# Which engine waits for the landing of the output: GpSimd or SyncE, in a one-core decode kernel

## The chip, the cores and the metric

The kernel runs on one core of a Trainium2 chip and gives instructions to five engines: TensorE (PE), VectorE (DVE), ScalarE (ACT), GpSimd (POOL) and SyncE (SP). They run side by side: the busy times of the first four, 58.4, 44.2, 30.4 and 10.0 us in the profile below, add up to 143.0 us in a span of 77.6. Where one waits for another in this kernel, it waits for a semaphore, a counter that the other raises; SyncE's longest such wait is 28.5 us. The metric is the device time of one execution in microseconds; quoted times are medians of several executions. Before the change it is 79.57 us (three runs, 79.53 to 79.73).

Besides the device time there is a profile. Its "span" runs from the first to the last of the kernel's own instructions that were recorded. The device time is about 2 us longer than the span (79.66 us against 77.6 in the profiled run), and this case is about those 2 us.

## The reference

One decode step: a layer norm, then an attention over a window of 4096 cached positions and a gated feed-forward block, both added to the input. Cut to what matters:

```python
x  = A_x                                  # 1 x 1 x 512, bf16
xn = _layernorm(x)
q  = xn @ wq                              # 32 heads of 128
scores = q @ k_cache[last 4096].T * Dh**-0.5
o  = softmax(scores) @ v_cache[last 4096] # 8 kv heads, each used by 4 heads
a  = o @ wo                               # 512 numbers
b  = xn + ((silu(xn @ w_gate) * (xn @ w_up)) @ w_down) * sigmoid(xn @ w_r)
return x + a + b                          # 1 x 1 x 512: 1 KB
```

About 30.7 MB are read from memory and 1 KB is written.

## The kernel before

The change touches only the last line of the body. This is the helper that gives waits to engines (cut), the helper that issues a transfer, and the end of the kernel:

```python
class Eng:
    ...
    def need(self, *toks):               # this engine waits for each (semaphore, value)
        for t in toks:
            ...
                self.e.wait_ge(sem, n)

    def dma(eng, name, out_, in_):
        s = S("d_" + name)
        ins = eng.dma_start(out=out_, in_=in_)
        ins.then_inc(s, 16)              # 16: the value that need() waits for
        ...
        return (s, 16)
    ...
    t_a = PE.mark(ins)                   # the last matrix product
    DVE.need(t_a)
    ACT.need(t_a)
    s_res = S("s_res")
    ve.tensor_copy(out=res[:, 0:HD], in_=g_ps[0]).then_inc(s_res, 1)
    ac.copy(out=res[:, HD:], in_=g_ps[1]).then_inc(s_res, 1)
    sy.wait_ge(s_res, 2)
    t_out = dma(sy, "out", out.rearrange("a b d -> (a b) d"), res)
    POOL.need(t_out)                     # keeps the kernel open until the output has landed
```

The framework's usual closing barrier is moved by this kernel to an early place in each engine's stream (a function `hoist`, not shown): in the trace GpSimd's semaphore instructions for it stand at 6.37 to 6.90 us of the span. So at its end an engine just falls through its last branch, which I call the **closing branch**. The wait of the last line is compiled into the closing branch of the engine that has it: in the trace this branch of GpSimd, with the wait on it, runs from 77.559 to 77.592 us, behind the landing at 77.534.

Of the kernel before, what the change touches and what calls it, by code (L numbers as in the profile page):

```python
# [38 lines left out]
def kernel(  # L39
# [63 lines left out]
    def early(eng, name, out_, in_):  # L103
# [81 lines left out]
    PE, ACT, DVE, POOL, SP = (Eng(nc, nc.tensor, "pe"), Eng(nc, nc.scalar, "act"), Eng(nc, nc.vector, "dve"),  # L185
                              Eng(nc, nc.gpsimd, "pool"), Eng(nc, nc.sync, "sp"))
# [10 lines left out]
# [3 lines that stand above are left out]
        ins.then_inc(s, 16)  # L200
        if name == "v0":
            ends(ins)
        return (s, 16)
# [365 lines left out]
    ac.copy(out=res[:, HD:], in_=g_ps[1]).then_inc(s_res, 1)  # L569
    sy.wait_ge(s_res, 2)  # L570
    t_out = dma(sy, "out", out.rearrange("a b d -> (a b) d"), res)
    POOL.need(t_out)


# [28 lines left out]
```

## Time and profile before

| | before |
|---|---|
| device time, median of 3 | 79.57 us |
| device time of the profiled run | 79.66 us |
| span of the profiled run | 77.6 us |
| from issue to landing of the output | 1.12 us |
| from landing to the end of device time | 2.13 us |

The last two rows are from the trace's records of semaphore updates. The store's semaphore is updated twice, at 76.851 and 77.534; the later one, 25 ns ahead of the branch that waits for it, is what I call the landing. In the profile's page, the first lines give each engine's busy time, with its share of the span, and what the transfers moved in 40 slices of the span:

```profile
PE 58.4 (75%) x642; PEld 30.6 (39%) x642; DVE 44.2 (57%) x96; ACT 30.4 (39%) x41; POOL 10.0 (13%) x22
...
DMA  6999999999999999999999999999999999989900
...
DMA packets 2745, 30.72 MB, mean 396 GB/s; under 512 B 307, under 2 KB 438, under 8 KB 822
```

The transfers fill 37 slices of 40, and GpSimd, with 13%, is the least busy engine. The last 1.2 us of the span, as busy time of each engine in two windows, show that nothing works there any more:

```profile
76.40:77.00 0.60, 0.00 (x0) 0.00 (x0) 0.00 (x0) 0.00 (x0) 0.00 (x0) 1.00 0.00 0
77.00:77.60 0.60, 0.00 (x0) 0.00 (x0) 0.00 (x0) 0.00 (x0) 0.00 (x0) 1.00 0.01 2
```

The columns are the window, its length, busy time and number of instructions of PE, PEld, DVE, ACT and POOL, then the granted clock, the transfers' share and GB/s.

### The profile page before, as it was taken

What the parts mean: (1) busy time and instruction counts of PE and PEld (TensorE: products, weight loads), DVE (VectorE), ACT (ScalarE), POOL (GpSimd) and SP (SyncE); (2) the same over time, 40 slices, a digit from 0 to 9 for tenths busy, and PEclk for the clock granted to TensorE, in tenths of its full rate; (3) what the DMA queues carried; (4) which work ended last, traced back from release to release, by engine and by line L of the source; (5) the groups of instructions that cost most, each with busy time, mean ns of one, the idle gap of its engine ahead of it and who ended that gap; (6) DMA issues with size and microseconds to landing.
All of it is one profiled execution on the core that took longest, in us unless ns stands there. A gap on an engine that the chain in (4) does not pass through costs nothing.

```text
span 77.6 us, 1640 instructions
## 1 busy us (share of the span) xinstructions
PE 58.4 (75%) x642; PEld 30.6 (39%) x642; DVE 44.2 (57%) x96; ACT 30.4 (39%) x41; POOL 10.0 (13%) x22
## 2 busy tenths in 40 slices
PE   0010797759997997997996796677887889898891
PEld 0010401346785575765864234222222344243240
DVE  2763910177656956868883652989879545600302
ACT  2760101404397698599568016143333322000001
POOL 3950000001020210201205900000000000000000
PEclk9999999999999999999999999999999999999999
DMA  6999999999999999999999999999999999989900
GB/s 136 405 406 422 414 422 427 422 469 414 439 456 439 405 422 414 439 439 431 405 410 422 481 414 422 413 449 399 451 406 451 413 422 414 481 361 413 355 29 1
DMA packets 2745, 30.72 MB, mean 396 GB/s; under 512 B 307, under 2 KB 438, under 8 KB 822
## 3 DMA queue, kind: packets, MB, share of 16 engines
q1 hardware_dynamic: 2738, 30.67, 94.0%
q8 instruction: 2, 0.03, 0.2%
q14 instruction: 1, 0.01, 0.0%
q10 hardware_dynamic: 4, 0.00, 0.0%
HBM read 30.67 MB, written 0.00 MB: 395 GB/s over the span
## 4 chain that ended last, share of the span: by engine, by line
DMA 64%; PE 20%; ACT 6%; DVE 4%; issue 2%; SPq 1%
DMA k_sb<-in_B_w_down_dram 50%; DMA wq_sb<-in_A_wq_dram 14%; PE ps L367 10%; ACT kT L342 6%; PE ps L541 3%; PE ps L376 3%; PE ps L295 2%; DVE kin L334 2%; PE ps L307 1%; SPq L199 1%; DVE kT L339 1%; DVE qpad L312 1%; DVE kT L568 1%; SPq L84 0%; SPq L101 0%
## 5 line engine op out<-in xcount | busy, mean ns | idle before, releaser
L342 ACT COPY kT<-ps 128x1024 bf16<-128x1024 bf16 x19 | 18.6, 1016 | 9.5 <-PE ps L367 9.4
L367 PE MATMUL ps<-perm_bf,kin 128*128 128x128 bf16 x256 | 18.7, 231 | 1.5 <-DVE kin L334 1.0
L367 PEld LDWEIGHTS ps<-perm_bf,kin 128*128 128x128 bf16 x256 | 15.8, 104 | 5.9 <-issue 4.7
L334 DVE COPY kin<-k_sb 128x2048 bf16<-128x2048 bf16 x16 | 10.9, 687 | 2.6 <-PE ps L367 2.6
L339 DVE COPY kT<-ps 128x1024 bf16<-128x1024 bf16 x13 | 9.0, 692 | 4.4 <-PE ps L367 3.8
L462 ACT CAST pvS<-ps 128x512 bf16<-128x512 f32 x8 | 4.7, 586 | 10.0 <-PE ps L468 10.0
L376 PE MATMUL ps<-kT,qAB 128*32 128x512 bf16 x68 | 7.1, 407 | 1.9 <-ACT kT L342 1.9
L191 PE MATMUL ps<-zmov,zst 128*128 128x512 bf16 x32 | 7.9, 381 | 0.0
L327 POOL COPY qAB<-qpad 128x64 bf16<-128x64 bf16 x8 | 3.6, 445 | 32.6 <-PE ps L376 32.6
L442 DVE COPY vin<-v_sb 128x2048 bf16<-128x2048 bf16 x8 | 5.5, 685 | 1.1 <-PE ps L477 0.9
L448 DVE COPY vin<-v_sb 128x2048 bf16<-128x2048 bf16 x8 | 5.5, 683 | 0.0
L477 PE MATMUL ps<-vin,pTcur 128*32 128x512 bf16 x32 | 3.2, 386 | 2.6 <-ACT pvS L462 2.2
L569 ACT CAST kT<-ps 1x256 bf16<-1x256 f32 x1 | 0.4, 362 | 11.4 <-PE ps L541 11.4
L489 PE MATMUL ps<-zmov,zst 128*128 128x512 bf16 x16 | 4.7, 376 | 0.0
L295 PE MATMUL ps<-wq_sb,xnT 128*1 128x512 bf16 x32 | 3.8, 620 | 0.6 <-DMA wq_sb<-in_A_wq_dram 0.6
L191 PEld LDWEIGHTS ps<-zmov,zst 128*128 128x128 bf16 x32 | 2.7, 97 | 3.7 <-issue 1.3
L251 PE MATMUL ps<-ident_bf,xn_row 1*128 1x1 bf16 x4 | 0.3, 166 | 5.2 <-DVE xn_row L246 5.2
L312 DVE COPY qpad<-ps 128x16 bf16<-128x16 bf16 x4 | 0.5, 170 | 5.4 <-PE ps L307 5.4
L555 DVE TENSOR_TENSOR kT<-ps,kT 128x512 f32<-128x512 f32 x1 | 0.7, 692 | 5.0 <-PE ps L536 5.0
L376 PEld LDWEIGHTS ps<-kT,qAB 128*32 128x32 bf16 x68 | 1.9, 93 | 4.1 <-issue 1.8
L477 PEld LDWEIGHTS ps<-vin,pTcur 128*32 128x32 bf16 x32 | 1.1, 93 | 6.0 <-DVE vin L442 5.5
L483 PE MATMUL ps<-vin,pTcur 128*32 128x512 bf16 x32 | 3.2, 387 | 0.3 <-DVE vin L448 0.2
(96 smaller groups left out, 54.7 us busy)
## 6 DMA issues: line engine op xcount, KB each, us to landing
v_sb<-in_A_v_cache_dram SPq DMA_DIRECT2D x4, 2048.0 KB, 38.2
k_sb<-in_A_k_cache_dram SPq DMA_DIRECT2D x3, 2048.0 KB, 23.3
wq_sb<-in_A_wq_dram SPq DMA_DIRECT2D x2, 2048.0 KB, 9.1
k_sb<-in_A_wo_dram SPq DMA_DIRECT2D x2, 2048.0 KB, 34.7
k_sb<-in_A_k_cache_dram SPq DMA_DIRECT2D x2, 1024.0 KB, 13.9
wq_sb<-in_B_w_gate_dram SPq DMA_DIRECT2D x1, 1792.0 KB, 43.0
wq_sb<-in_B_w_up_dram SPq DMA_DIRECT2D x1, 1792.0 KB, 46.9
k_sb<-in_B_w_down_dram SPq DMA_DIRECT2D x1, 896.0 KB, 38.7
```

The lines of the kernel that those rows point to most:

```text
L191: te.matmul(ps[:, 7, :], lhsT=zst[:], rhs=zmov[:], start=True, stop=True)
L295: ins = te.matmul(ps[32 * c:32 * c + 1, hf, :], lhsT=xnT[:, kt:kt + 1], rhs=wq_sb[:, kt, (4 * hf + c) * 512:(4 * hf + c + 1) * 512], start ...
L334: ve.tensor_copy(out=kin[:, 2 * h:2 * h + 2, :], in_=k_sb[:, g, 2 * h:2 * h + 2, :]).then_inc(s_c[h], 1)
L339: ve.tensor_copy(out=kT[:, b, :], in_=tp[:, b, :]).then_inc(s_ev[b], 1)
L342: ac.copy(out=kT[:, b, :], in_=tp[:, b, :]).then_inc(s_ev[b], 1)
L367: ins = te.transpose(tp[:, b, k * P:(k + 1) * P], kin[:, b, k * P:(k + 1) * P], perm_bf[:])
L376: ins = te.matmul(sc[32 * cq:32 * cq + 32, e, :], lhsT=qAB[:, e, :], rhs=kT[:, b, :].rearrange("d (k h q) -> d h k q", h=2, q=PH)[:, e], s ...
L442: ve.tensor_copy(out=vin[:, 0].rearrange("p (q k) d -> p q (k d)", q=4), in_=v_in[:, :, 0:4 * DH]).then_inc(s_va, 1)
L448: ve.tensor_copy(out=vin[:, 1].rearrange("p (q k) d -> p q (k d)", q=4), in_=v_in[:, :, 4 * DH:]).then_inc(s_vb, 1)
L462: ac.copy(out=pvS[:].rearrange("p t d -> p (t d)"), in_=pv_ps).then_inc(s_pvs, 1)
L477: ins = te.matmul(pv_ps[32 * tl:32 * tl + 32, :], lhsT=pTcur[:, tl].rearrange("p q e r -> p (q e r)"), rhs=vin[:, 0].rearrange("p (q t) d ...
L489: te.matmul(ps[:, 7, :], lhsT=zst[:], rhs=zmov[:], start=True, stop=True)
```

## The change

The intent: let SyncE, which issues the store, also wait for it, and leave GpSimd free to end.

```diff
     sy.wait_ge(s_res, 2)
     t_out = dma(sy, "out", out.rearrange("a b d -> (a b) d"), res)
-    POOL.need(t_out)
+    SP.need(t_out)
```

## The prediction

In what follows the first barrier is the first nine updates of semaphore 2 at the kernel's end and the second barrier the last nine; a step is one of these updates, a hop the time from one to the next, and an engine's ending is the time from its closing branch to its own step. That the first five of nine belong to one engine each was my reading.

> **What bounds the kernel now.** I first read the head of the profile page and its chain of waits, to see whether the line that changes lies in the part that costs time.
>
> ```profile
> span 77.6 us, 1640 instructions
> ...
> DMA 64%; PE 20%; ACT 6%; DVE 4%; issue 2%; SPq 1%
> ```
>
> Most of the 77.6 us goes to loading 30.7 MB. The diff touches none of that. It moves one wait, the one that holds the kernel open until its 1 KB output has landed, so what counts is the last two microseconds. The timeline from 74 us on ends with these lines (start in us, length in us, engine, line, what it writes and reads, and in brackets the idle time before it):
>
> ```profile
> 75.97 0.36 ACT L569 CAST kT<-ps 1x256 bf16<-1x256 f32 x1 [11.42 <-PE ps L541]
> 75.97 0.41 DVE L568 CAST kT<-ps 1x256 bf16<-1x256 f32 x1 [2.96 <-PE ps L541]
> 76.41 0.32 SPq L199 DMA_DIRECT2D out_dram<-kT  x1
> ```
>
> Two casts finish at 76.33 and 76.38, SyncE then spends 0.32 us issuing the store, and nothing else is shown although the span runs on to 77.6. The reader is to see a tail in which every compute engine is idle: whatever is saved or added there comes off the time one for one. Next I asked what GpSimd, the holder of the wait, and SyncE do late in the kernel. GpSimd's timeline ends with
>
> ```profile
> 43.49 0.52 POOL L405 MEMSET kT<- 128x512 f32 x1
> 44.08 0.60 POOL L407 COPY kT<-resid 1x512 f32<-1x512 f32 x1
> ```
>
> so it has been idle from 44.7 us and only stands at the wait. SyncE's list of waits has as its longest
>
> ```profile
> SPq L199 <- DVE kT L568: 28.5, 1, 28.5
> ```
>
> which is 28.5 us of waiting for the last cast before it issues the store. Both engines have nothing else to do at the end.
>
> The lines above do not show the landing, so I read the trace's raw records of semaphore updates, transfers and branches. Times are from the span's start. The store's packet starts at 77.159, takes 46 ns, and its semaphore receives two updates, at 76.851 and at 77.534. GpSimd's closing branch, which carries the wait, runs from 77.559 to 77.592, and that is the end of the span. The records then go on past the span. Semaphore 2, which the kernel does not use, counts nine updates: 76.114, 76.453, 78.214, 78.259, 78.282, 78.384, 78.423, 78.457, 78.504. [...] semaphore 2 then counts nine again, from 79.297 to 79.662. The profiled run took 79.66 us. So the device time covers this ending too, and the 2.07 us between 77.59 and 79.66 have to be part of the estimate.
>
> [...]
>
> **The change part by part.** The order of instructions is the same on all five engines: all that happens in the built program is that the condition "output semaphore reaches 16" leaves GpSimd's closing branch and goes onto SyncE's closing branch, directly behind the store. No instruction is added. Issue and landing cannot move, since SyncE has already issued when it begins to wait.
>
> Waking up: GpSimd's branch starts 25 ns after the landing (77.559 less 77.534). SyncE started the store 17 ns after its own last semaphore update (76.413 less 76.396). Estimate: 8 ns saved.
>
> The engine's own ending: [...] The first two steps of the first barrier, 76.114 and 76.453, come 165 ns after PE's last update (75.949) and 110 ns after ACT's (76.343); the third step is 1.76 us late, and only GpSimd's branch is so late. So the third step is GpSimd's, and its ending takes 78.214 − 77.592 = 0.622 us, all of it exposed. SyncE is not among the first two, whose steps come before its store is even issued at 76.735; so it is the fourth or fifth, and I take the fifth[...]. Its ending, x, lies today beside the landing of the store and is hidden; after the change GpSimd's is hidden and x is exposed.
>
> The barrier: today it resumes at step three and reaches step five 68 ns later (78.282 − 78.214). With SyncE last, the first four steps are done before it arrives. So 68 ns disappear.
>
> Sum: step five is now at 78.282; afterwards at 77.592 − 0.008 + x. What follows it, 79.662 − 78.282 = 1.38 us, is unchanged. The gain is 0.698 − x. Nothing here measures x. If SyncE's ending were as long as GpSimd's, 0.622, the gain is 0.08 us.[...] the two other endings that can be read are 0.11 and 0.165[...]. I choose x = 0.42, about midway between 0.622 and that pair with a little weight to the long side. Gain 0.28 us: 79.57 − 0.28 = 79.29, say 79.3.
>
> **The rivals.** First: SyncE's ending is longer, because this engine has issued nearly all DMAs and may have more to close. The trace bounds it. Its step follows the fourth by 23 ns in the first barrier and also in the second, so it was ready by about 78.259, at most 1.524 us after its store was issued (76.735). With x = 1.524 the result is 0.83 us slower, 80.40, or +1.0%. For it: so many DMA issues on that queue. Against it: the other known endings are far shorter. Second: x is near zero and the gain is 0.69 us, 78.88, or −0.9%. For it: the first barrier hops pass SyncE in 23 ns. Against it: GpSimd's branch alone takes 33 ns[...]. Third: the ending[...] equals GpSimd's; then only the hops and the waking are won, 79.49, which three runs that spread from 79.53 to 79.73 would barely show. Fourth: a wait directly behind the issue on the queue's own sequencer delays the landing.[...]; I give this no time.
>
> **Range and chances.** The bounds 78.88 and 80.40 are both within 1.59 us (2%) of 79.57, so leaving the 2% band would take something that the end of the kernel doesn't contain, such as another speed of the loads. Eight in ten: x between 0.08 and 0.75 us, which is 78.95 to 79.62, with some room for the spread between runs upwards: 78.95 to 79.75. Chances: faster by over 2% 0.01, within 2% 0.98, slower by over 2% 0.01.
>
> **What would show each step.** In the changed kernel's profile the closing branch that ends the span should be SyncE's, about 20 ns after the landing, and the landing should still be about 0.8 us after the issue ended. The span should stay at 77.6. Semaphore 2 should have four of its nine updates before 77.5 (the third now long before, at GpSimd's leisure) and the fifth at x after the branch, and 1.38 us should follow. If GpSimd's step still comes late, the chain is in another order than I read. If the gain sits within the span, or the time moves by over 1%, the bound from the endings is wrong.

## The result

The changed kernel takes 79.16 us (median of five runs, 78.91 to 79.23); the kernel before, 79.57 us (five runs, 79.40 to 79.73). The ratio is 0.9937, 95% interval 0.9912 to 0.9962: 0.6% faster, clear of noise, inside the 2% band. A ratio here is the mean time of one kernel's runs over that of the other's of the same rounds, so it is not quite the ratio of the medians.

The head of the page, and the transfers, after:

```profile
span 77.7 us, 1640 instructions
...
PE 56.4 (72%) x642; PEld 29.7 (38%) x642; DVE 43.9 (57%) x96; ACT 30.4 (39%) x41; POOL 10.3 (13%) x22
...
DMA packets 2745, 30.72 MB, mean 395 GB/s; under 512 B 307, under 2 KB 438, under 8 KB 822
...
PE 42%; DMA 27%; ACT 14%; DVE 9%; issue 3%; SPq 2%; DVEq 0%
```

The span did not get shorter (77.6 before, 77.7 after), with the same instructions and bytes. The chain of waits, the last line, looks different: before, it went from the end straight back to the load of the last weights; now it goes back mostly through matrix products and evictions. The change isn't what did that. This profile was recorded with 0.978 of TensorE's clock granted, the one before with 1.000. Of the 14 kept profiles the only other one at 0.978, after_again below, has the same chain line; in the twelve at 1.000 transfers make up 63% or more, and in after_third, which is the changed kernel too, the line is nearly that of before:

```profile
DMA 63%; PE 21%; ACT 6%; DVE 4%; issue 2%; SPq 1%
```

The tail after the last cast is the same at both clocks (below: 1.587 and 1.589 us from landing to last update), so the clock does not bear on the gain. The end of the timeline after:

```profile
76.13 0.36 ACT L569 CAST kT<-ps 1x256 bf16<-1x256 f32 x1 [10.27 <-PE ps L541]
76.13 0.41 DVE L568 CAST kT<-ps 1x256 bf16<-1x256 f32 x1 [2.45 <-PE ps L541]
76.57 0.32 SPq L199 DMA_DIRECT2D out_dram<-kT  x1
```

It has the same three entries with the same durations, all 0.16 us later because the body of this execution took that much longer. What is new stands in the list of SyncE's waits (who waited for whom, us in total, times, longest). Its first lines before, and then after:

```profile
SPq L199 <- DVE kT L568: 28.5, 1, 28.5
SPq L199 <- DVE kin L334: 17.9, 1, 17.9
SPq L199 <- PE ps L295: 3.4, 1, 3.4
SPq L84 <- PEq L84: 0.5, 2, 0.4
```

```profile
SPq L199 <- DVE kT L568: 28.5, 1, 28.5
SPq L199 <- DVE kin L334: 19.0, 1, 19.0
SPq L199 <- PE ps L295: 2.5, 1, 2.5
SPq L101 <- DMA out_dram<-kT: 0.8, 1, 0.8
```

The last line, the closing branch waiting 0.8 us for the output, is not in SyncE's list before. So the wait moved and the span stayed; the gain must lie after the span, where the profile's views show nothing. The trace's record of semaphore updates goes on there. Semaphore 2, which the kernel doesn't use, is updated nine times and later nine times again. I call the two groups barriers, since in the experiments below each of the first five updates of the first group comes late when one engine does, a different engine for each. From its third update on, the second group before runs like the first, to within 4 ns (45, 23, 106, 38, 34 and 47 ns against 45, 23, 102, 39, 34 and 47). From 78.399, just behind the sixth update of the first group, to 79.073 the trace before has updates of 244 other semaphores, once each, in five blocks of ascending numbers from 7 to 255. Times in us from the span's start:

| | before | after |
|---|---|---|
| output issued | 76.413 | 76.573 |
| output landed | 77.534 | 77.698 |
| closing branch with the wait | GpSimd, 77.559 to 77.592 | SyncE, 77.714 to 77.747 |
| first barrier, updates 1 and 2 | 76.114, 76.453 | 76.275, 76.616 |
| update 3 | **78.214** | 76.654 |
| update 4 | 78.259 | 76.700 |
| update 5 | 78.282 | **77.965** |
| updates 6 to 9 | 78.384, 78.423, 78.457, 78.504 | 78.008, 78.047, 78.081, 78.128 |
| second barrier, first and last update | 79.297, 79.662 | 78.921, 79.285 |
| from landing to last update | 2.128 | 1.587 |

Bold is the update that came late, and to the engine that waits it belongs: the third is GpSimd's, the fifth SyncE's. From its closing branch to its own update GpSimd needs 0.622 us and SyncE 0.218. The stretch from landing to last update shrank by 0.541 us.

The device times of these two profiled runs, 79.66 and 79.16, are not the last update alone: the first equals it, the second is 0.125 us below it. Of the 14 kept profiles six have a device time that equals the last update, and eight one that is 0.115 to 0.128 us below it; both cases occur with the changed kernel itself (79.03 against a last update at 79.153; 79.04 against 79.040). I could not find what decides, so I do not build on single device times. The mean of device time less span (the spans are rounded to 0.1 us) removes the body's scatter: it is 1.98 to 2.02 us for the kernel before in the rounds of the four batches of experiments, and 1.50, 1.49 and 1.49 us for the changed kernel in its three sets of runs. That is about 0.5 us of difference, in agreement with the ratio (0.63% of 79.57 is 0.50 us).

### The profile page after: what moved, and what is told of

Read it like the earlier page. It is cut to its first block, busy times and chain, and to the rows that moved or that the text cites.

```text
span 77.7 us, 1640 instructions
## 1 busy us (share of the span) xinstructions
PE 56.4 (72%) x642; PEld 29.7 (38%) x642; DVE 43.9 (57%) x96; ACT 30.4 (39%) x41; POOL 10.3 (13%) x22
## 4 chain that ended last, share of the span: by engine, by line
PE 42%; DMA 27%; ACT 14%; DVE 9%; issue 3%; SPq 2%; DVEq 0%
DMA k_sb<-in_A_k_cache_dram 27%; PE ps L367 13%; ACT kT L342 8%; PE ps L191 7%; PE ps L376 5%; ACT pvS L462 5%; PE ps L541 3%; PE ps L483 3%; PE ps L477 3%; PE ps L536 2%; DVE vin L448 2%; ACT kin L425 2%; PE ps L511 2%; SPq L199 2%; PE ps L468 2%
## 5 line engine op out<-in xcount | busy, mean ns | idle before, releaser
L367 PE MATMUL ps<-perm_bf,kin 128*128 128x128 bf16 x256 | 18.1, 227 | 4.0 <-DVE kin L334 3.6
L367 PEld LDWEIGHTS ps<-perm_bf,kin 128*128 128x128 bf16 x256 | 15.2, 101 | 8.4 <-issue 4.4
L295 PE MATMUL ps<-wq_sb,xnT 128*1 128x512 bf16 x32 | 2.9, 499 | 0.8 <-DMA wq_sb<-in_A_wq_dram 0.8
L447 DVE COPY pTcur<-ps 128x256 bf16<-128x256 bf16 x8 | 2.3, 285 | 1.6 <-PE ps L431 1.6
```

The source lines that it names most:

```text
L367: ins = te.transpose(tp[:, b, k * P:(k + 1) * P], kin[:, b, k * P:(k + 1) * P], perm_bf[:])
```

## The experiments

The theory: the device time goes on until the barriers after the kernel are through. From its closing branch every engine takes a time of its own, its **ending**, until its update in the first barrier, and it has a fixed place there (PE, ACT, POOL, DVE, SP; with one of them late, 0, 1, 2, 3 and 4 updates stand before the late one in pe, act, before, dve and after). The wait for the output decides whose ending is exposed and how much of the barrier is left after it. Rivals: the landing itself comes, or is noticed, sooner when the issuing engine waits; GpSimd's ending is long only because the engine had been idle since 44.7 us; SyncE's is short only because it had just issued the store; or all engines that compute (the expectations say: with a datapath) have a long ending.

Twelve runs were made, of nine new kernels, the changed kernel twice more and one of the nine again, each over five rounds and with correct results. The kernels and medians come first; the pieces, from the traces, are in the table at the end of this section.

The ratios of the first three batches are blurred by some longer runs. Six of the 33 runs of the kernel before in these batches, two of act, two of poolwarm and one each of storeact2 and poolnops ran with 0.978 of the clock granted and a span 0.6 to 1.0 us over the median of the others. The ratios below include them. The clock figure alone is not the reason: three runs of the changed kernel and one of best were at 0.978 too, with spans of 77.6 or 77.7 us as usual. With the twelve long runs left out (a selection made afterwards) the ratios of the means are: both 1.001, act 0.996, dve 0.996, pe 0.997, poolwarm 1.001, spnops 0.999, poolnops 0.993, storeact 0.993, storeact2 0.992, and the changed kernel 0.994 twice. That is the order of the traces, but for differences of 0.001.

**Both engines wait (both).**

```diff
+    POOL.need(t_out)
     SP.need(t_out)
```

> GpSimd and SyncE both wait for the landing. Theory (the later of the engines' own endings sets the barrier): the endings run side by side, GpSimd's 0.62 us is exposed again, the barrier resumes at its third step about 0.65 us after the landing and the fifth follows 0.07 us later; time as before the change, ratio 0.998 to 1.002. Rival A (the landing is seen faster or comes faster when SyncE waits for its own store): the gain stays, ratio about 0.994. Rival B (two waits on one semaphore add): slower than before, ratio over 1.003.

Measured: 79.69 us against 79.67, ratio 0.9988 (0.9939 to 1.0037), an interval that overlaps the changed kernel's; the trace decides. SyncE's list of waits in this run has its line:

```profile
SPq L101 <- DMA out_dram<-kT: 0.8, 1, 0.8
```

So SyncE waits exactly as in the changed kernel, and the gain is gone. GpSimd's ending is again 0.622 us, and the landing is followed by 2.128 us, the number of the kernel before to the nanosecond. The first rival falls: it isn't what SyncE does that gains, it is that GpSimd isn't last.

**One of the other three waits (act, dve, pe).**

```diff
-    SP.need(t_out)
+    ACT.need(t_out)      # act;  DVE.need(t_out) in dve;  PE.need(t_out) in pe
```

> ScalarE alone waits. Theory: ScalarE is the second in the barrier, so exactly one update of the barrier's semaphore stands before the late one, and from the late one to the ninth it takes about 0.33 us (0.16 with SyncE). With an ending of about 0.22 us like SyncE's the time is about 0.17 us over the changed kernel, ratio to before about 0.996. Rival (every engine with a datapath has an ending of about 0.6 us like GpSimd's): ratio 1.000 or above.

> VectorE alone waits. Theory: fourth in the barrier, three updates before the late one, about 0.25 us from it to the ninth; with an ending of 0.22 to 0.28 us[...] about 0.15 us over the changed kernel, ratio to before about 0.996. Rival (every engine with a datapath has a long ending): ratio 0.999 to 1.001.

> TensorE alone waits. Theory: first in the barrier, no update before the late one, about 0.36 us from it to the ninth; with an ending of 0.22 us about 0.2 us over the changed kernel, ratio to before about 0.997. Rival (long endings on every engine with a datapath): ratio 1.001.

Measured: act 79.31 us, ratio 0.9968 (0.9913 to 1.0023); dve 79.22, 0.9927 (0.9878 to 0.9976); pe 79.34, 0.9939 (0.9890 to 0.9988). The intervals are wide because of the long runs (three of the 11 of the kernel before and two of act, each 0.6 to 0.8 us over the median of the others), and dve and pe lie below the expected 0.996 and 0.997; without the long runs they are at these values. The order of these three is read from their traces. The updates ahead of the late one are one, three and none, as expected: the places in the barrier are those of the prediction. The endings are 0.203, 0.265 and 0.198 us. So the rival of a long ending on every engine that computes falls: of the five endings only GpSimd's, 0.622, is long. TensorE misses the expectation in one item: its closing branch took 182 ns where the others took 33 to 47, so landing to ninth update is 0.34 us over the changed kernel and not about 0.2. In act the stretch from the ninth update to the last was 1.242 us instead of 1.158; it reappears once below. The extra time lies ahead of the updates of semaphores 7 to 53, the last to begin of the five blocks ahead of the second barrier: 0.314 us after the ninth update in act and 0.221 in the kernel before; its cause is left open.

**GpSimd waits, but has just worked (poolwarm).**

```diff
-    SP.need(t_out)
+    POOL.need(t_a)
+    gp.memset(junk2[:], 0.0)     # 1 x 2 elements; junk2 is allocated further up
+    POOL.need(t_out)
```

> GpSimd waits as before the change, but does a tiny memset after the last matrix product, some 1.5 us ahead of the landing, so it has not been idle since 44.7 us. Theory[...]: GpSimd's ending stays 0.62 us, ratio 0.998 to 1.002. Rival (the long ending is a cold start after 30 us of idleness): the ending falls to 0.2 to 0.4 us, ratio 0.995 to 0.997.

Measured: 79.68 us against 79.60, ratio 1.0037 (0.9984 to 1.0090), above the expected 1.002 because of its two long runs. The end of GpSimd's timeline in this run:

```profile
43.60 0.60 POOL L408 COPY kT<-resid 1x512 f32<-1x512 f32 x1
75.83 0.09 POOL L574 MEMSET junk<- 1x2 f32 x1 [31.62 <-PE ps L542]
```

The engine worked 1.5 us before the landing at 77.362, and its ending is 0.623 us. The cold start falls; why GpSimd's ending is so long no run here shows.

**Ten more instructions, on SyncE behind the wait (spnops) and on GpSimd beside it (poolnops).**

```diff
     SP.need(t_out)                       # spnops
+    s_n = S("s_n")
+    for _ in range(10):
+        sy.sem_inc(s_n, 1)
```
```diff
+    s_n = S("s_n")                       # poolnops
+    POOL.need(t_a)
+    for _ in range(10):
+        gp.sem_inc(s_n, 1)
     SP.need(t_out)
```

> SyncE waits as in the changed kernel, then runs ten increments of an unused semaphore before its closing branch. Theory: SyncE's instructions behind the wait are exposed one for one;[...] 0.5 to 0.65 us are lost and the time comes back to that of before, ratio 0.999 to 1.003. Rival (something else than SyncE sets the end): ratio stays at 0.994.

> As the changed kernel, but GpSimd runs ten increments of an unused semaphore after the last matrix product, about 0.6 us of its sequencer, the same that cost time on SyncE. Theory (GpSimd is off the path after the change): its step comes about 1.2 us after the last product, still ahead of SyncE's, and the time is that of the changed kernel, ratio about 0.993. Rival (GpSimd's ending still holds the barrier): ratio 0.997 or above.

Measured: spnops 79.45 us against 79.60, ratio 0.9972 (0.9933 to 1.0012), below the expected 0.999, and 2.041 us from landing to last update. In SyncE's list of waits the wait now stands on the first increment:

```profile
SPq L575 <- DMA out_dram<-kT: 0.8, 1, 0.8
```

The increments follow each other every 61 ns on average, and the last ends 562 ns after the first begins. The loss is 0.454 us and not that much, because behind the last increment the fifth update came after 0.136 us, where the changed kernel spends 0.033 on the branch and 0.218 behind it. Poolnops: 79.04 us against 79.63, ratio 0.9941 (0.9898 to 0.9983). There the increments are 79 ns apart, GpSimd's update comes 1.31 us after the last product, at 77.116, and SyncE's at 77.657 with the same 0.218 us ending. What costs 0.45 us on SyncE costs nothing that can be seen on GpSimd (79.04 us, the changed kernel of this batch 79.07): after the change GpSimd is off the path. This run also shows GpSimd's long way into the barrier with nothing waiting on its branch: from its last increment to its update it took 0.561 us, where SyncE in spnops took 0.136.

**The changed kernel again (after_again, after_third).** No edit; yardsticks of the second and third batch.

> The changed kernel once more, as the yardstick of this batch: ending of SyncE 0.22 us, ratio to before about 0.994.

> The changed kernel as the yardstick of this batch: ratio to before about 0.993, 1.59 us from the landing to the last update of the barrier's semaphore.

Measured: 79.05 us, ratio 0.9924 (0.9886 to 0.9962), and 79.07 us, ratio 0.9929 (0.9899 to 0.9959). The ending was 0.218 us both times.

**ScalarE issues the store, SyncE waits (storeact, storeact2).**

```diff
-    sy.wait_ge(s_res, 2)
-    t_out = dma(sy, "out", out.rearrange("a b d -> (a b) d"), res)
+    ac.wait_ge(s_res, 2)
+    t_out = dma(ac, "out", out.rearrange("a b d -> (a b) d"), res)
     SP.need(t_out)
```

> ScalarE issues the store, SyncE waits for it. Theory: SyncE's ending does not depend on having issued the store just before, 0.22 us as in the changed kernel, ratio 0.993 to 0.996, any difference lying between the casts and the landing. Rival (SyncE's ending is short because it is still in the code of its own store, or because it waits for its own queue): the ending grows by 0.1 us or more.

> The version with the store issued by ScalarE and awaited by SyncE, once more beside the changed kernel. If its shorter issue (0.23 us against 0.32) is what brought it 0.07 us, it is again 0.04 to 0.1 us below the changed kernel of this batch; if that was noise, the two lie within 0.03 us or change places.

Measured: 78.96 us, ratio 0.9917 (0.9878 to 0.9956), and 78.92 us, 0.9928 (0.9890 to 0.9965; one of six runs at 0.978 of the clock, 79.58). From the first run's list of SyncE's waits and its timeline:

```profile
SPq L101 <- DMA out_dram<-kT: 29.6, 1, 29.6
```
```profile
76.35 0.23 ACTq L199 DMA_DIRECT2D out_dram<-kT  x1
```

SyncE stood at its closing branch for 29.6 us and hadn't issued anything since the weights; its ending is 0.210 us. So its short ending isn't owed to the store just issued. The issue on ScalarE took 0.23 us where SyncE took 0.32, and issue to landing 1.079 and 1.090 us where the changed kernel has 1.121 to 1.125. The traces give 0.04 to 0.05 us less from issue to ninth update. The runs do not measure that: the medians lie 0.09 and 0.15 us under those of the changed kernel in the same batches, the mean of storeact2 with its long run 0.03 us under. Neither figure of storeact2 is in the expected 0.04 to 0.1 us, and storeact's ratio is below its expected 0.993.

**The wait on an increment ahead of the branch, and the store on ScalarE (best).** What spnops showed by the way was worth a kernel.

```diff
     ...                                  # as in storeact
     SP.need(t_out)
+    sy.sem_inc(S("s_n"), 1)
```

> ScalarE issues the store, and SyncE's wait stands on one increment of an unused semaphore ahead of the closing branch, not on the branch. With ten increments the barrier's fifth step came 0.136 us after the last increment, against 0.033 for the branch and 0.218 behind it in the changed kernel; if a branch that stands at a wait costs the difference, one increment brings the landing to the ninth update in about 0.33 us instead of 0.43, and the last update about 1.49 us after the landing; time 78.85 us, ratio to before about 0.991. Rival[...]: the fifth step comes as late as in the changed kernel or later, 1.58 us or more from the landing to the last update, ratio about 0.992.

Measured: 78.90 us (78.67 to 78.97) against 79.64, ratio 0.9896 (0.9878 to 0.9914). SyncE's list of waits has the wait where it should be:

```profile
SPq L573 <- DMA out_dram<-kT: 29.6, 1, 29.6
```

Landing to ninth update is 0.331 us, the expected 0.33: an instruction more, and 0.09 us less than storeact's 0.42. In its profiled run the extra 0.085 us between the ninth and the last update, seen in act, ate most of it again (1.573 us in all, and not the expected 1.49). It can't have done so in all six runs: their mean of device time less span fell to 1.36 us, from 1.44 to 1.46 in storeact and storeact2, although the span now ends 0.016 us sooner after the landing (with a 17 ns increment and not with a 33 ns branch). This version beats both kernels in its medians; its interval and the changed kernel's (0.9899 to 0.9959 in the batch before) just overlap. SyncE's closing branch is still in the program of best, but without a wait, and the trace has no record of it. Why the branch costs more when the wait stands on it is not shown.

The pieces, all in nanoseconds from the trace of each kernel's profiled run:

| kernel | waits | landing to branch | branch | ending | updates before | its update to ninth | landing to ninth |
|---|---|---|---|---|---|---|---|
| before | GpSimd | 25 | 33 | 622 | 2 | 290 | 970 |
| both | GpSimd (and SyncE) | 25 | 33 | 622 | 2 | 289 | 969 |
| poolwarm | GpSimd | 24 | 33 | 623 | 2 | 289 | 969 |
| pe | TensorE | 29 | 182 | 198 | 0 | 362 | 771 |
| act | ScalarE | 21 | 33 | 203 | 1 | 328 | 585 |
| dve | VectorE | 28 | 47 | 265 | 3 | 245 | 585 |
| changed | SyncE | 16 | 33 | 218 | 4 | 163 | 430 |
| storeact | SyncE | 17 | 33 | 210 | 4 | 163 | 423 |
| spnops | SyncE | 17, then 698 to its update | | | 4 | 165 | 880 |
| best | SyncE | 17, then 151 to its update | | | 4 | 163 | 331 |

From the ninth update to the last it is 1151 to 1161 ns in all of them, but 1242 in act and best.

## Why the prediction was right

The prediction was 79.3 us with a range of 78.95 to 79.75; 79.16 came out. The mechanism was right: the gain is GpSimd's ending exchanged for SyncE's, behind the span. The size was not: it forecast a gain of 0.28 us, and the traces show 0.54, the ratio 0.50. The range held because it allowed SyncE's ending x anything from 0.08 to 0.75 us. Point by point:

- **The body.** "Issue and landing cannot move": right. Issue to landing is 1.121 us before and 1.125 after, and the span is 77.6 and 77.7.
- **Waking.** 8 ns were estimated; 25 less 16 is 9.
- **GpSimd's ending of 0.622 us, all exposed.** Right, and shown by both and poolwarm, which put it back.
- **SyncE's place in the barrier.** I took the fifth; the trace of the kernel before did not tell it from the fourth. Four updates stand before the late one in every kernel in which SyncE waits last, and with none, one and three before it pe, act and dve confirm the other places.
- **SyncE's ending x.** This is the mis-sized term. The prediction chose 0.42 us, weighting between GpSimd's 0.622 and the two short endings; it measured 0.218, on the side of the other engines. The two readings 0.110 (ScalarE) and 0.165 (TensorE) were nearer but too short: when these engines wait, in act and pe, their endings are 0.203 and 0.198. With x = 0.218 its own sum, 0.698 − x, gives 0.48 us.
- **"What follows it, 1.38 us, is unchanged."** Wrong by 0.06 us. When SyncE comes last, the sixth update follows the fifth after 43 ns; when it is not last, after 102. In dve, whose engine gives the fourth update late, it is also 102, and with ScalarE or TensorE last too. A reading that fits all of them is that the sixth update comes no sooner than some 125 ns after the fourth, VectorE's; with SyncE last the fourth is long past (76.700, the sixth 78.008). The 125 ns are my estimate, from 78.259 and 78.384 in the kernel before; no run isolates it. It adds 0.059 to 0.48: 0.54, the 0.541 of the traces.
- **The rivals.** A longer ending of SyncE (80.40), an ending near zero (78.88) and one equal to GpSimd's (79.49) are refuted by the 218 ns. A delay of the landing by the wait behind the issue did not occur. The bound of −0.9% to +1.0% held, and so did the chance of 0.98 for "within 2%".

## What to carry to other kernels

A wait that keeps a kernel open was not free to stand anywhere just because its engine was idle: GpSimd had had no work since 44.7 us, and moving the wait from it to SyncE gained 0.5 us. On the path were the engine's ending after the wait (0.198 to 0.622 us) and the rest of the first barrier behind it (0.163 us with SyncE last, 0.362 with TensorE). Give the wait to the engine with the shortest remainder; here that is SyncE, with 430 ns from landing to ninth update, and GpSimd, with 970, is the worst of five by 0.2 us over the next one (TensorE, 771). When a change moves the device time (here 79.57 to 79.16 us) and not the span (77.6 and 77.7), read the semaphore updates behind the span before looking for a cause within it.
